# Partial sums copied into PSUM banks a stage earlier, and the w_down pieces made at other places, in a four-layer Fourier-mixing and GEGLU kernel

## The chip, the cores and the metric

The kernel runs on one core of a Trainium2 chip. The metric is the device time of one execution in microseconds; the time before is the median of three runs, 1634.65 us (1634.25 to 1635.71). The profile is of one more execution, which took 1635.97 us; from its first to its last instruction there are 1634.0 us (the span), and the mean granted TensorE clock was 0.996.

## What is computed

The input x has 2048 rows of 512 numbers. Four layers follow one another; layers 0 and 2 mix, layers 1 and 3 are a GEGLU block. The same weights serve both layers of a kind, and everything is float32.

```python
# mix (layers 0, 2), on z = layernorm(x)
a = z @ dft_hid_re.T;  b = z @ dft_hid_im.T
x = x + (dft_seq_re @ a - dft_seq_im @ b)
# GEGLU (layers 1, 3), on z = layernorm(x)
x = x + (gelu(z @ w_gate) * (z @ w_up)) @ w_down
```

dft_seq is 2048 x 2048 (real and imaginary part), dft_hid 512 x 512, w_gate and w_up 512 x 1792, w_down 1792 x 512.

## The kernel before

**Products.** A float32 operand is divided into two parts: the high part is a copy rounded to fp32r on ScalarE (L148), the low part is the difference on VectorE (L150). A product is three matmuls, high by high, high by low and low by high (`mm3`, L205, L206, L207). Only the first matmuls of layer 0 take plain float32 (L797). Large products are done in two-by-two blocks with seven block products in place of eight. For that, sums and differences of the operands are formed on VectorE (`minus` L181, `plus` L188 from SBUF), they are divided into high and low part, and the results are combined as they leave their PSUM banks: `plus` on VectorE (L185) or a copy on ScalarE (`copied`, L192). There are eight banks. Where a result begins with a sum that is known already, a bank is filled with it first: the seed, a ScalarE copy into the bank (`seed`, L199), and the matmuls add to it.

**A mix layer** has four blocks b of 512 output rows. Per block the stages are A11, A12 (two of the seven products over the sequence, 8 steps k each), S2 (products T2, T1 and T3, each a little behind the one before), the hidden-layer groups, S4 (products B22 and T4), and more hidden-layer groups (MID_HID, LATE_HID). `plan` lists the stages: A11 of all four blocks, A12 of all four, then per block S2, EARLY_HID, S4, MID_HID, LATE_HID. A stage's product with one k is `six` (six matmuls); the weights come from a stream of items through `take`, which loads and divides some items ahead. A12 begins with the seed of two banks by A11's sums; S2 begins with the seed of two banks by the sums of A11 for its block, which for b > 0 were put into DRAM and are loaded back by `fetch_sums`; the hidden-layer groups begin with the seed of four banks by the rows of x (`x_seeded`), to which the layer's result is added.

**A GEGLU layer** has two halves w of 1024 rows. It runs 14 passes n over gate and up columns (`up`), each with seven products; every pass forms h, and two passes make one pair k = 0..6 of w_down rows. The w_down products A11 and A12 of a pair are done in the passes (`beside`), the other five (S1, S2, S3, S4, A22) after them, in the order of `down_order`: the late products. In layers 1 (both halves) and 3 (first half) all seven pairs are done in this way; in layer 3's second half five pairs, and the rest by plain products.

**w_down pieces.** The w_down operands of a pair k are made once and kept in DRAM. `weight_steps` gives six steps for it: a load (L922 to L924, 0.52 MB), the sums (four of 128x256 on VectorE), and four divides (three of 128x512 and one of 128x256, on ScalarE and VectorE), whose results POOL's queue writes out (seven writes of 256 KB, L309 and L943). Seven pairs make 42 steps. The gate/up pieces are made in the same way in layer 1's first passes.

**What sets the order.** Instructions are issued per engine in a static order that a scheduler of the framework makes from the program's order and its own estimates. Some steps are hung onto it by hand: `step()` runs after each product, takes one entry from `queue`, and each `pace[0]`-th time one from `slow`. With `in_order` set (in the mix layers, but for layer 0's A11 and A12), splits, differences and seeds are issued behind the last bank read on their engine (`behind`, L141). Loads are on SP's queue, most writes on POOL's. Tiles of SBUF come from 98 slots; a load waits until the earlier reader of its slot is done.

The lines that the prediction names: L148 and L150 splits, L181 and L188 differences and sums, L192 and L185 bank reads, L199 seeds, L205 to L207 matmuls, L309 and L943 writes of pieces.

Of the kernel before, what the change touches and what calls it, by code (L numbers as in the profile page):

```python
# [20 lines left out]
NB = S // TB  # L21
NT = TB // P
# [7 lines left out]
LAG = 6  # L30
NEAR = 3, 2, 6
EARLY = 2
PACE = 9
SKEW = 2, 1
NSLOT = 98
SEVEN = {(1, 0): 7, (1, 1): 7, (3, 0): 7, (3, 1): 5}
FORE = {0: 4, 2: 4}
MADE = 5
LEAD = 3
NK = NS // 2  # L40
DOWN_PACE = 4


@with_exitstack
def fnet_geglu(ctx: ExitStack, tc: tile.TileContext, x_in, ws, wh, wgu, wdn, wdc, out):
# [86 lines left out]
    sb = Slots(slots, "s", NSLOT)  # L132
# [125 lines left out]
        for i in range(NT):  # L258
            xrows[b, i] = x_load(layer, b * NT + i)

    def x_seeded(b):

        banks = [ps8.get() for _ in range(NT)]
        for i, ps in enumerate(banks):
            t = xrows.pop((b, i))
            seed(ps, t)
            sb.put(t)
        return banks

# [175 lines left out]
    NP = NF // 2  # L445

    def down_order(layer, w):
        n = SEVEN[layer, w]
        up = [(name, k) for k in range(n) for name in ("A11", "A12")]
        if n < NP:  # L450
            late = [("S2", k) for k in range(n)] + [("S1", 0)] + [("S3", k) for k in range(n)] + [("S1", 1)]
            late += [("A22", k) for k in range(n - 1)] + [("S1", k) for k in range(2, n)]
            return up, late + [("A22", n - 1)] + [("S4", k) for k in range(n)]
        late = [("S1", k) for k in range(LEAD)] + [up.pop()]
        late += [p for k in range(n) for p in [("S2", k)] + [("S1", k + LEAD)] * (k + LEAD < n)]
        late += [("S4", k) for k in range(2)]
        for k in range(2, n):
            late += [("S3", 3 * (k - 2) // 2 + i) for i in range(1 + k % 2) if 3 * (k - 2) // 2 + i < n] + [("S4", k)]
        return up, late + [("A22", k) for k in range(n)]
# [47 lines left out]
                items.extend((F32, (wdn[f],), plain, None) for f in range(2 * SEVEN[layer + 1, w], NF))  # L507


    queue, slow, steps_done, pace = [], [], [0], [PACE]  # L510

    def step():
        if queue:
            run = queue.pop(0)
            if run is not None:
                run()
        steps_done[0] += 1
        if slow and steps_done[0] % pace[0] == 0:
            slow.pop(0)()


# [212 lines left out]
    def mix(layer):  # L734
# [14 lines left out]
        def hid_groups(b, groups):  # L749

            first, last = b not in hid, groups is LATE_HID
            if first:
                hid[b] = x_seeded(b)
                chores.extend(chores_at(b))
                hid_left[0] = 2 * ND
            if last and b + 1 < min(NB, FORE[layer]):
                fetch_sums(b + 1)  # L760
            for n, g in enumerate(groups):
                (hi, lo), w = take()
                for i in range(NT):
# [3 lines left out]
                step()  # L767
                for _ in range(-(-len(chores) // hid_left[0]) if chores else 0):
                    chores.pop(0)()
                hid_left[0] -= 1  # L770
            if last:
                for i, ps in enumerate(hid.pop(b)):
                    x_out(layer, b * NT + i, ps)

        def six(ps, name, k, start, stop, done=None):
            w = take()
# [14 lines left out]
        def a11(b):  # L791
            chain = [ps8.get() for _ in range(2)]
            for k in range(NK):
                if bare(layer, b, "A11", k):
                    t, = take()
                    for c in range(2):
                        nc.tensor.matmul(chain[c], za[k][:, c * P:(c + 1) * P], t, start=k == 0, stop=False, skip_group_check=True)  # L797
                    sb.put(t)
                    step()
                else:  # L800
                    six(chain, "B11", k, k == 0, k == NK - 1, "11" if b == NB - 1 else None)
            sums[b] = [copied(p) for p in chain]
            ps8.put(*chain)

        def a12(b):
            stream["more"] = 0
            if layer and b == 0:
                lend("x")
                lend("z")
            side = [ps8.get() for _ in range(2)]  # L810
            for c in range(2):
                seed(side[c], sums[b][c])
                if b:
                    put_away((layer, b, c), sums[b][c])
            for k in range(NK):
                six(side, "B21", k, False, k == NK - 1, "21" if b == NB - 1 else None)
            for c in range(2):
# [9 lines left out]
        def s2(b):  # L827
# [3 lines left out]
                lend("x")  # L831
            cs.update(cs_next)
            cs_next.clear()
            chain = [ps8.get() for _ in range(2)]
            for c in range(2):
                seed(chain[c], sums[b][c])
            sb.put(*sums.pop(b))
            x_banks(layer, b)
            one, three = [ps8.get() for _ in range(2)], [ps8.get() for _ in range(2)]
            sides[b] = one, three  # L840
# [2 lines left out]
            for i, k in skewed(3):  # L843
                if i == 0:
                    six(chain, "T2", k, False, k == NK - 1)
                elif i == 1:
                    six(one, "T1", k, k == 0, k == NK - 1, "T12" if last else None)
                else:
                    six(three, "T3", k, k == 0, k == NK - 1)
                if k < NK - 1:  # L850
                    continue
                if i == 0:
                    us[b] = [copied(p) for p in chain]
                    ps8.put(*chain)
                for c in range(2):
                    if i == 1:
                        v = cs[1, 2 + c] = sb.get()
                        plus(v, us[b][c], one[c])
                    elif i == 2:
                        plus(cs[1, 2 + c], cs[1, 2 + c], three[c])  # L860

        def s4(b):
# [5 lines left out]
            for i, k in skewed(2):  # L868
# [3 lines left out]
                    six(three, "T4", k, False, k == NK - 1, "T34" if last else None)  # L872
                if k < NK - 1:
                    continue
                for c in range(2):
                    if i == 0:
                        v = cs[0, 2 + c] = sb.get()
# [7 lines left out]
        for n, (b, what) in enumerate(plan(layer)):  # L885
# [17 lines left out]
        pace[0] = PACE  # L903

# [78 lines left out]
    def geglu(w, layer):  # L983
# [475 lines left out]
```

## Time and profile before

| | before |
|---|---|
| time, median of 3 runs | 1634.65 us |
| the profiled execution: time, span | 1635.97 us, 1634.0 us |
| TensorE busy | 1605.1 us (98%) |
| VectorE busy | 1135.9 us (70%) |
| ScalarE busy | 888.8 us (54%) |
| GpSimd busy | 269.3 us (16%) |
| DMA | 419.14 MB, mean 257 GB/s |
| matmuls | 7008 |

Times in the trace count from the span's start. The stages lie there as follows: layer 0 has A11 and A12 until about 96 us, block 0 until 175, block 1 until 252, block 2 until 328, block 3 until 413. Layer 1's first half has its passes until 569, its second half until 776; layer 2's A11 run from 811 to 864, its A12 to 920, its blocks to 1224; layer 3 takes the rest.

The rows of busy time overlap, since the engines work beside each other. A row of the list of waits reads: engine and its line, the line it waited for, total us, number of times, longest. A row of a table of stretches reads: from and to, length, then for PE, PEld (the weight loads of TensorE), DVE (VectorE), ACT (ScalarE) and POOL (GpSimd) the busy us and the number of instructions, the granted clock, the DMA engines' share and GB/s. A row of a timeline reads: start, duration, engine, line, operation, and in brackets the idle time ahead of it with what ended it. A row of groups reads: line, engine, operation, tiles, shapes, count, busy us and mean ns of one, then idle us ahead of them.

### The profile page before, as it was taken

What the parts mean: (1) busy time and instruction counts of PE and PEld (TensorE: products, weight loads), DVE (VectorE), ACT (ScalarE), POOL (GpSimd) and SP (SyncE); (2) the same over time, 40 slices, a digit from 0 to 9 for tenths busy, and PEclk for the clock granted to TensorE, in tenths of its full rate; (3) what the DMA queues carried; (4) which work ended last, traced back from release to release, by engine and by line L of the source; (5) the groups of instructions that cost most, each with busy time, mean ns of one, the idle gap of its engine ahead of it and who ended that gap; (6) DMA issues with size and microseconds to landing.
All of it is one profiled execution on the core that took longest, in us unless ns stands there. A gap on an engine that the chain in (4) does not pass through costs nothing. (4 is left out here: it accounts for less than half of the span.)

```text
span 1634.0 us, 22639 instructions
## 1 busy us (share of the span) xinstructions
PE 1605.1 (98%) x7008; PEld 1318.0 (81%) x7008; DVE 1135.9 (70%) x1958; ACT 888.8 (54%) x1711; POOL 269.3 (16%) x469
## 2 busy tenths in 40 slices
PE   9999999989999999999998999999999999999998
PEld 7887888868888887788786788888888888888886
DVE  7997888878787784445977958777863447744573
ACT  8855475645676653546656634655555536433460
POOL 4112131342544101100040000101401000000001
PEclk9999999999999999999999999999999999999999
DMA  9878899997988889955794776868999676895445
GB/s 359 291 260 302 314 322 316 329 327 236 307 292 255 275 277 304 252 180 174 255 302 140 257 241 206 307 203 303 257 298 308 205 213 204 275 300 187 123 148 155
DMA packets 258840, 419.14 MB, mean 257 GB/s; under 512 B 28512, under 2 KB 106592, under 8 KB 257696
## 3 DMA queue, kind: packets, MB, share of 16 engines
q1 hardware_dynamic: 234480, 336.16, 64.9%
q0 software_dynamic: 24240, 81.55, 13.8%
q8 instruction: 55, 0.90, 0.2%
q14 instruction: 65, 0.53, 0.1%
HBM read 341.31 MB, written 76.28 MB: 256 GB/s over the span
## 5 line engine op out<-in xcount | busy, mean ns | idle before, releaser
L206 PE MATMUL p<-s,s 128*128 128x512 f32 x2320 | 903.3, 390 | 2.4 <-DVE s L150 2.4
L207 PE MATMUL p<-s,s 128*128 128x512 f32 x2320 | 896.5, 390 | 0.0
L205 PE MATMUL p<-s,s 128*128 128x512 f32 x2320 | 871.9, 391 | 18.8 <-ACT s L148 9.0
L150 DVE TENSOR_TENSOR s<-s,s 128x512 fp32r<-128x512 f32 (+1 forms) x806 | 507.7, 665 | 127.8 <-ACT s L148 108.7
L148 ACT ACTIVATE s<-s 128x512 fp32r<-128x512 f32 (+1 forms) x806 | 452.4, 606 | 222.6 <-DVE s L181 63.9
L205 PEld LDWEIGHTS p<-s,s 128*128 128x128 f32 x2320 | 436.4, 188 | 115.6 <-ACT s L148 11.8
L206 PEld LDWEIGHTS p<-s,s 128*128 128x128 f32 x2320 | 436.5, 188 | 95.7 <-DVE s L150 5.5
L207 PEld LDWEIGHTS p<-s,s 128*128 128x128 f32 x2320 | 436.7, 188 | 90.8
L185 DVE TENSOR_TENSOR s<-s,p 128x512 f32<-128x512 f32 x196 | 132.6, 683 | 205.8 <-PE p L207 163.7
L181 DVE TENSOR_TENSOR s<-s,s 128x512 f32<-128x512 f32 (+1 forms) x364 | 217.9, 615 | 5.4 <-DMA s<-ws 3.0
L192 ACT ACTIVATE s<-p 128x512 f32<-128x512 f32 x233 | 133.9, 593 | 114.5 <-PE p L207 112.0
L980 ACT ACTIVATE s<-s 128x512 f32<-128x512 f32 x84 | 52.8, 630 | 71.5 <-DVE s L185 70.8
L564 POOL TENSOR_SCALAR rstd<-rstd 128x1 f32<-128x1 f32 x40 | 30.6, 764 | 281.1 <-ACT s L563 266.2
L148 ACT ACTIVATE s<-xwide 128x512 fp32r<-128x512 f32 x73 | 44.7, 625 | 49.7 <-DVE xwide L185 25.9
L994 DVE TENSOR_TENSOR s<-s,p 128x512 f32<-128x512 f32 x56 | 38.4, 685 | 34.6 <-PE p L207 31.7
L309 POOL DMA_DIRECT2D wb<-s x84 | 45.8, 546 | 94.3 <-ACT s L148 70.5
L980 ACT ACTIVATE s<-p 128x512 f32<-128x512 f32 x28 | 16.7, 598 | 76.3 <-PE p L207 72.5
L150 DVE TENSOR_TENSOR s<-xwide,s 128x512 fp32r<-128x512 f32 x73 | 49.6, 688 | 10.9 <-ACT s L148 10.0
L188 DVE TENSOR_TENSOR s<-s,s 128x512 f32<-128x512 f32 (+1 forms) x72 | 43.5, 610 | 17.2 <-DMA s<-ws 15.9
L587 ACT ACTIVATE s<-s,shift,rstd 128x512 f32<-128x512 f32 x56 | 45.0, 811 | 14.5 <-DVE shift L554 8.9
L199 ACT ACTIVATE p<-p 128x512 f32<-128x512 f32 x56 | 32.7, 584 | 36.4 <-PE p L207 27.6
L669 DVE STREAM_TRANSPOSE wide<-s 128x512 f32<-128x512 f32 x27 | 19.1, 709 | 36.3 <-ACT s L587 36.3
(104 smaller groups left out, 603.5 us busy)
## 6 DMA issues: line engine op xcount, KB each, us to landing
s<-ws SPq DMA_DIRECT2D x380, 256.0 KB, 5.3
s<-wb SPq DMA_DIRECT2D x294, 256.0 KB, 4.5
s<-wc SPq DMA_DIRECT2D x182, 256.0 KB, 4.0
s<-wh SPq DMA_DIRECT2D x118, 256.0 KB, 5.3
wb<-s POOLq DMA_DIRECT2D x98, 256.0 KB, 4.5
s<-x SPq DMA_DIRECT2D x60, 256.0 KB, 5.3
xwide<-ws SPq DMA_DIRECT2D x52, 256.0 KB, 5.0
wc<-s POOLq DMA_DIRECT2D x49, 256.0 KB, 4.7
```

Of the source, the lines that this page charges most:

```text
L148: newest["ACT"] = nc.scalar.activation(hi, src, AF.Copy)
L150: newest["DVE"] = nc.vector.tensor_tensor(lo, src, f32(hi), op=ALU.subtract)
L181: nc.vector.tensor_tensor(out, a, b, op=ALU.subtract)
L185: bank_read["DVE"] = nc.vector.tensor_tensor(out, a, b, op=ALU.add)
L188: nc.vector.tensor_tensor(out, a, b, op=ALU.add)
L192: bank_read["ACT"] = nc.scalar.activation(v, src, AF.Copy)
L205: nc.tensor.matmul(ps, ah, bh, start=start, stop=False, skip_group_check=True)
L206: nc.tensor.matmul(ps, ah, bl, start=False, stop=False, skip_group_check=True)
L207: nc.tensor.matmul(ps, al, bh, start=False, stop=stop, skip_group_check=True)
L309: nc.gpsimd.dma_start(a, f32(t))
L587: nc.scalar.activation(z, x, AF.Identity, bias=shift, scale=rstd)
L980: nc.scalar.activation(t, g, AF.Gelu_apprx_tanh)
```

## The change

Three things are done.

1. Seeds. The seeds of A12 and S2 move out of these stages into the stage before. `a12_seeded(b)` fills two banks: for block 0 at step k = 3 (SEED_AT) of the last A11, for block b + 1 at step 3 of A12 of block b. `s2_seeded(b)` does so for S2: for block 0 at step 3 of the last A12, for later blocks in the last hidden-layer group of the block before; the loads of `fetch_sums` come one group earlier. `x_seeded` fills its four banks in two halves, two at step 3 of T2 in S2, two after T2's banks are copied.
2. w_down pieces. The 42 steps are no longer in `slow`. Four of them run ahead of T2's bank read and four ahead of B22's bank read in layer 0's blocks 0, 1 and 2 (24 steps, the pieces of four pairs), none in block 3, and two in each pass n > 2 of layer 1's first half (18 steps, three pairs).
3. Late w_down operands. In the passes from n = 9 on, where all seven pairs are done, the operands of the first entries of the late list (two more with each pass) are divided already if their pair is there. The last A12 stands two places later in the late list.

```diff
+EARLY_FROM, EARLY_EACH = 8,2
-DOWN_PACE = 4
+SEED_AT = 3
+DOWN_RUNS = ((0,0,0,0),(4,4,4,0),(4,4,4,0),2)
...
-    def x_seeded(b):
-        banks = [ps8.get() for _ in range(NT)]
-        for i, ps in enumerate(banks):
+    def x_seeded(b, rows):
+        banks = []
+        for i in rows:
             t = xrows.pop((b, i))
-            seed(ps, t)
+            banks.append(ps8.get())
+            seed(banks[-1], t)
             sb.put(t)
...
-        late = [("S1", k) for k in range(LEAD)] + [up.pop()]
+        late = [("S1", k) for k in range(LEAD)]
         late += [p for k in range(n) for p in [("S2", k)] + [("S1", k + LEAD)] * (k + LEAD < n)]
+        late.insert(LEAD + 2, up.pop())
...
             if first:
-                hid[b] = x_seeded(b)
+                hid[b] = hid_banks.pop(b)
...
-            if last and b + 1 < min(NB, FORE[layer]):
-                fetch_sums(b + 1)
+            if b + 1 < NB:
+                if groups is MID_HID:
+                    fetch_sums(b + 1)
+                elif last:
+                    s2_seeded(b + 1)
...
+        def down_pieces(b, at):
+            for _ in range(DOWN_RUNS[at][b]):
+                if layer == 0 and down_making:
+                    down_making.pop(0)()
...
+                if b == FORE[layer] - 1 and k == SEED_AT:
+                    a12_seeded(0)
...
+        def a12_seeded(b):
+            side_banks[b] = [ps8.get() for _ in range(2)]
+            for c in range(2):
+                seed(side_banks[b][c], sums[b][c])
+                if b:
+                    put_away((layer, b, c), sums[b][c])
+
+        def s2_seeded(b):
+            chain_banks[b] = [ps8.get() for _ in range(2)]
+            for c in range(2):
+                seed(chain_banks[b][c], sums[b][c])
+            sb.put(*sums.pop(b))
...
-            side = [ps8.get() for _ in range(2)]
-            for c in range(2):
-                seed(side[c], sums[b][c])
-                if b:
-                    put_away((layer, b, c), sums[b][c])
+            side = side_banks.pop(b)
             for k in range(NK):
                 six(side, "B21", k, False, k == NK - 1, "21" if b == NB - 1 else None)
+                if k == SEED_AT:
+                    if b + 1 < FORE[layer]:
+                        a12_seeded(b + 1)
+                    else:
+                        s2_seeded(0)
...
-            chain = [ps8.get() for _ in range(2)]
-            for c in range(2):
-                seed(chain[c], sums[b][c])
-            sb.put(*sums.pop(b))
+            chain = chain_banks.pop(b)
...
+                if i == 0 and k == SEED_AT:
+                    hid_banks[b] = x_seeded(b, range(2))
...
                 if i == 0:
+                    down_pieces(b, 1)
                     us[b] = [copied(p) for p in chain]
                     ps8.put(*chain)
+                    hid_banks[b] += x_seeded(b, range(2, NT))
...
+                if i == 0:
+                    down_pieces(b, 2)
...
-                pace[0] = DOWN_PACE
                 for k in range(NP):
                     load, making = down_weight_steps(k)
-                    slow.extend([load] + making)
+                    down_making.extend([load] + making)
...
+            if n > 2:
+                for _ in range(DOWN_RUNS[3]):
+                    if down_making:
+                        down_making.pop(0)()
             product(n, chain[n], "S2", "T2", False, True)
...
+            if pairs == NP:
+                for name, k in down_order(layer, w)[1][:max(0, n - EARLY_FROM) * EARLY_EACH]:
+                    if k in h4:
+                        prepared(name, k)
             product(n, chain[n], "A22", "T4", False, True)
```

More of the change, by code (lines that the diff above doesn't have):

```diff
@@ L507, in fnet_geglu @@
                 items.extend((F32, (wdn[f],), plain, None) for f in range(2 * SEVEN[layer + 1, w], NF))
-    queue, slow, steps_done, pace = [], [], [0], [PACE]
+    queue, slow, steps_done, down_making = [], [], [0], []
     def step():
@@ L517, in step @@
         steps_done[0] += 1
-        if slow and steps_done[0] % pace[0] == 0:
+        if slow and steps_done[0] % PACE == 0:
             slow.pop(0)()
@@ L767, in hid_groups @@
                 step()
+                down_pieces(b, 0)
                 for _ in range(-(-len(chores) // hid_left[0]) if chores else 0):
@@ L801, in a11 @@
                     six(chain, "B11", k, k == 0, k == NK - 1, "11" if b == NB - 1 else None)
+                if b == FORE[layer] - 1 and k == SEED_AT:
+                    a12_seeded(0)
             sums[b] = [copied(p) for p in chain]
             ps8.put(*chain)
+        side_banks, chain_banks, hid_banks = {}, {}, {}
+        def a12_seeded(b):
[9 more added lines that the diff above has]
+            sb.put(*sums.pop(b))
         def a12(b):
@@ L902, in mix @@
         in_order[0] = False
-        pace[0] = PACE
     wblocks = {n: dram.tile([P, 7 * 512], F32, name=f"wb{n}") for n in range(NF)}
```

## The prediction

> **What bounds the kernel now.** I read the page's engine table first, then TensorE's list of waits, and then cut the span into the stretches where TensorE stands.
>
> ```profile
> span 1634.0 us, 22639 instructions
> PE 1605.1 (98%) x7008; PEld 1318.0 (81%) x7008; DVE 1135.9 (70%) x1958; ACT 888.8 (54%) x1711; POOL 269.3 (16%) x469
> ```
>
> TensorE is busy 98% of the span, and the change takes no matmul away. So only time in which TensorE stands or runs at a lower clock can be won: 1634.0 - 1605.1 = 29 us of idle time, and a little more around each gap, as the next rows show. The list of waits names what it stands for:
>
> ```profile
> PE p L205 <- ACT s L148: 9.0, 7, 2.6
> PE p L205 <- ACT p L199: 8.0, 4, 4.1
> ```
>
> L199 is the seed, a copy of known sums into a PSUM bank ahead of the products that add to it; four waits of 8.0 us in all are for it. L148 is the high part of a split. This is the table of stretches that hold the gaps; its columns are the stretch, its length, busy time and count for PE, PEld, DVE, ACT and POOL, the granted clock, the DMA share and GB/s.
>
> ```profile
> 128.00:135.00 7.00, 4.70 (x20) 3.35 (x19) 5.71 (x10) 6.25 (x13) 0.54 (x1) 1.00 0.51 170
> 340.00:360.00 20.00, 16.40 (x68) 12.15 (x68) 19.13 (x34) 9.58 (x16) 9.27 (x17) 1.00 0.99 313
> 360.00:376.00 16.00, 13.97 (x53) 10.61 (x52) 11.69 (x21) 9.30 (x18) 11.57 (x23) 0.89 0.88 240
> 651.00:658.00 7.00, 4.54 (x18) 2.80 (x18) 0.69 (x1) 7.00 (x23) 2.22 (x6) 1.00 1.14 243
> 777.00:800.00 23.00, 20.76 (x90) 16.34 (x89) 21.55 (x37) 15.66 (x29) 0.00 (x0) 1.00 0.77 254
> 863.00:880.00 17.00, 12.89 (x44) 10.11 (x43) 15.45 (x36) 8.33 (x16) 1.07 (x2) 0.80 0.29 93
> 880.00:894.00 14.00, 12.49 (x55) 10.01 (x54) 9.71 (x20) 8.48 (x16) 0.00 (x0) 1.00 0.38 126
> 894.00:906.00 12.00, 10.76 (x48) 8.60 (x47) 9.61 (x17) 8.48 (x16) 1.08 (x2) 1.00 0.87 279
> 906.00:920.00 14.00, 12.82 (x57) 10.26 (x57) 14.00 (x25) 8.56 (x16) 1.08 (x2) 1.00 0.79 253
> ```
>
> The first three are stages S2 and S4 of the first mix layer (layer 0), in blocks 0, 3 and 3. 651 to 658 lies in the gate/up passes of layer 1's second half, 777 to 800 in its late w_down products. The last four are the four A12 stages of layer 2. How much a gap costs is read from the largest, in TensorE's timeline (start, duration, idle before):
>
> ```profile
> 862.73 0.39 PE L205 MATMUL p<-s,s 128*128 128x512 f32 x1
> ...
> 863.86 0.39 PE L207 MATMUL p<-s,s 128*128 128x512 f32 x1
> 868.36 0.80 PE L205 MATMUL p<-s,s 128*128 128x512 f32 x1 [4.11 <-ACT p L199]
> 868.95 0.63 PE L206 MATMUL p<-s,s 128*128 128x512 f32 x1
> ...
> 874.50 0.43 PE L207 MATMUL p<-s,s 128*128 128x512 f32 x1
> 874.77 0.39 PE L205 MATMUL p<-s,s 128*128 128x512 f32 x1
> ```
>
> Ahead of the gap five starts take 1.13 us, 0.227 each. From 863.86 to 874.77 there are 16 starts, 3.6 us at that pace; they took 10.9. So 7.3 us are lost: 4.1 idle, 13 starts from 868.95 to 874.50 at 0.427 instead of 0.227 (2.6), and 0.6 for the pipeline's emptying and refilling. At full clock that last part is about 0.3 a gap, since a matmul lasts 0.39 and starts 0.227 apart, on both sides of the gap.
>
> **The change, part by part.** (1) Seeds of A12 and S2 a stage ahead. Why the wait of 4.1 us is there shows in ScalarE's timeline:
>
> ```profile
> 860.60 5.07 ACT L148 ACTIVATE s<-s 128x512 fp32r<-128x512 f32 x12
> ...
> 866.75 1.07 ACT L192 ACTIVATE s<-p 128x512 f32<-128x512 f32 x2
> 867.70 1.12 ACT L199 ACTIVATE p<-s 128x512 f32<-128x512 f32 x2
> ```
>
> A11 ended at 864.2, its bank copies (L192) stood behind splits until 866.75, and the next stage's seeds came behind the copies. In the new order the seeds of A12 block 0 need only A11 block 0, long done, and stand in the middle of A11 block 3; each next pair stands in the middle of the A12 before. The copies remain but nothing on TensorE waits for them until later. What goes: 7.3 us, and 1.51 + 0.3, 1.24 + 0.3, 1.18 + 0.3 in the next three rows (14.00 - 12.49 and so on), 4.8: **12.1 us**. The ten L199 instructions stay as many, so ScalarE's load is unchanged.
>
> What is late next is VectorE. The last four rows have 15.45 + 9.71 + 9.61 + 14.00 = 48.8 us of its work in 57; with 12.1 us out there are 44.9. If all that work were due inside the stretch, 3.9 us would come back; if enough of it is for stages after 920, none. The stretch behind has room:
>
> ```profile
> 924.00:944.00 20.00, 20.00 (x90) 16.55 (x89) 16.22 (x27) 7.78 (x15) 0.00 (x0) 1.00 0.70 228
> DVE s L150 <- ACT s L148: 5.7, 5, 2.9
> DVE s L188 <- DMA s<-ws: 2.3, 2, 2.1
> ```
>
> The two waits are VectorE's for 864 to 920. The 5.7 us are for ScalarE, which itself stands at bank reads behind TensorE; they go when TensorE doesn't stand. I take 1.0 of the 3.9, nearer the low end because the 14.00 of the last row holds splits for T1 and T2 that are used after 920. **Part 1: -11.1.**
>
> (2) Layer 0: w_down pieces out of block 3, hidden-layer seeds and S2's seeds earlier. VectorE is busy 19.13 of 20 us in 340:360, and ahead of that it had stood:
>
> ```profile
> 339.08 0.69 DVE L188 TENSOR_TENSOR s<-s,s 128x512 f32<-128x512 f32 x1 [4.04 <-DMA s<-ws]
> 340.71 0.69 DVE L188 TENSOR_TENSOR s<-s,s 128x512 f32<-128x512 f32 x1 [0.94 <-DMA s<-ws]
> 330.00:340.00 10.00, 10.00 (x46) 8.29 (x45) 4.81 (x8) 3.77 (x8) 0.57 (x2) 1.00 1.03 408
> L943 POOL DMA_DIRECT2D wc<-s x3: 539/539/539, 290.5 to 375.9; - x3
> ```
>
> Two sums came 5.0 us late for loads of the sequence weights, with the DMA engines full at 408 GB/s, and VectorE did not catch up before 360. The L943 row is of 252 to 413: three of seven w_down pieces are made in blocks 2 and 3. One piece is a load of 0.52 MB and seven writes of 256 KB, 2.36 MB; three are 7.1 MB and 15 steps on VectorE. By the order of the new kernel's instructions these are gone from the stretch, four pieces are made between blocks 0 and 2, ahead of bank reads at which VectorE waits anyway, and S2's first products don't wait for a seed. Lost now: 2.30 + 0.6 in 128:135; 3.60 + four gaps by 0.3 in 340:360; and in 360:376
>
> ```profile
> 366.90 0.73 PE L205 MATMUL p<-s,s 128*128 128x512 f32 x2 [1.21 <-ACT s L148]
> 368.45 0.49 PE L205 MATMUL p<-s,s 128*128 128x512 f32 x1 [0.83 <-ACT s L148]
> 369.54 0.63 PE L206 MATMUL p<-s,s 128*128 128x512 f32 x1
> 372.52 0.53 PE L207 MATMUL p<-s,s 128*128 128x512 f32 x1
> ```
>
> 2.03 + 0.6 and nine starts at 0.427 (1.8): 2.9 + 4.8 + 4.4 = 12.1. Bounds: nothing of it left, or only 128:135 won. S4 opens on splits that come behind S2's last bank reads in either kernel, so I leave 1.9 standing at that boundary. **Part 2: -10.2.**
>
> The Trainium skill, TensorE: Matmul & The Clock Gate, "What's actually happening", says that the clock is halved after at least one idle window of about 3.4 us. The trace agrees at 863.86 (4.11 us), but nine half-speed starts also followed 1.21 and 0.83 us of idle time. By the rule the 1.9 us left standing would stay 1.9; by these rows they could carry another 1.8.
>
> (3) Late w_down operands split in the passes, A12's last product two places later. 777:800 loses 23.00 - 20.76 = 2.2 of idle time in two gaps, 2.9 with refilling, while VectorE is busy 21.55 of 23. Ten splits of it move in front of 800, and further back. Between 0 and 2.9 I take 2.4. **Part 3: -2.4.** 651:658 (2.5 idle) waits for norm terms, which are unchanged: 0.
>
> (4) What comes into layer 1's first passes. Their rows, two passes each, and VectorE's and ScalarE's forms there:
>
> ```profile
> 439.70:461.40 21.70, 21.70 (x97) 17.98 (x96) 16.20 (x32) 14.56 (x32) 9.54 (x19) 1.00 1.04 361
> 461.40:483.20 21.80, 21.80 (x98) 18.06 (x97) 18.12 (x35) 15.12 (x32) 9.46 (x18) 1.00 0.77 275
> ...
> 526.70:548.50 21.80, 21.80 (x97) 18.05 (x97) 14.47 (x26) 11.38 (x21) 7.01 (x13) 1.00 1.02 325
> ...
> sum 129.00, PE 129.00 PEld 106.83 DVE 98.17 ACT 83.33 POOL 44.44; mean PE 21.50 PEld 17.80 DVE 16.36 ACT 13.89 POOL 7.41
> L150 DVE TENSOR_TENSOR s<-s,s 128x512 fp32r<-128x512 f32 x55 | 37.0, 689 | 25.3 <-ACT s L148 23.1 <-PE p L206 1.4 <-ACT s L980 0.7
> L181 DVE TENSOR_TENSOR s<-s,s 128x256 f32<-128x256 f32 x27 | 11.4, 421 | 0.2
> L148 ACT ACTIVATE s<-s 128x512 fp32r<-128x512 f32 x58 | 34.9, 623 | 7.0 <-DVE s L994 3.4 <-PE p L207 2.8 <-PE p L206 0.6
> ```
>
> TensorE never stands here now. A piece is four 256-wide sums (4 x 0.42), three 512-wide splits (3 x 0.69) and one 256-wide (0.42): 4.2 us of VectorE, and 2.3 of ScalarE. Three pieces and ten early splits (6.9 and 6.2) make VectorE 98.2 + 12.5 + 6.9 = 117.6 of 129 us (91%) and ScalarE 83.3 + 6.8 + 6.2 = 96.3 (75%). What hides them is VectorE's 31 us of idle time; 25.3 of it are waits for ScalarE's half of a split, and so not all free. The 21 writes stand on POOL's queue with the gate/up pieces' writes, and loads on SP's queue wait for the slots they free. 7.1 MB over nine passes of 10.9 us add 72 GB/s; the busiest row with new pieces, 526.70:548.50, goes from 325 to 397, under the 408 of 330:340. Bounds: 0, and 5.0, which is what late loads cost VectorE at 339 to 341, once. I take **+2**, between them.
>
> The Trainium skill, DMA: Bandwidth & Descriptors, "Where 436 GB/s comes from", says that the HBM side binds transfers between HBM and SBUF at about 358 GB/s a core. The trace shows 408 for 10 us, so I don't go by it; by it 39 GB/s over 21.8 us, 0.85 MB, would come 2.4 us late, and the sum would be that much worse.
>
> The sum: -11.1 - 10.2 - 2.4 + 2 = -21.7 against the profiled execution's own 1635.97 us (1634.0 of span and 2.0 around it), 1614.3. The median of the runs, 1634.65, is 1.3 lower, so I say **1613**.
>
> **Rivals.** (A) VectorE takes over in layer 2's A12 stages: the 3.9 us all come back, and the 2.3 of its load waits besides, 6.2 in place of 1.0: 1618. For it speak 14.00 of 14.00 in 906:920; against it the work that is due later. (B) The change does not do in block 3 what it says: the DMA engines, at shares of 0.88 to 1.03 from 330 to 376, are what is late, not VectorE's load, and the weights' sums wait all the same. Then of 9.2 us in 340:376 only some 3 go, 6 fewer with the left boundary counted once: 1619. Against it: 7.1 MB leave just these blocks. (C) Slower: the pieces in the passes find no slots. Their sums stand at VectorE's head waiting for a load that waits for POOL's writes, and the splits of the current pass stand behind them. The price a pass is that of 340:360, where 5.0 us of such waits became 4.8 on TensorE; nine passes, 43 us against 23.7 of gain: 1654. It decides from 2.6 us a pass. For it: DMA shares of 1.04 and 1.02 in two of the rows. Against it: VectorE's idle time of 31 us, and SP's order, which has each load about a pass ahead of its sums.
>
> **How the numbers follow.** Forecast 0.68, spread over 1606 to 1617: 1606 if parts 1 to 3 leave nothing standing and part 4 costs nothing (1634.65 - 27.2 = 1607, and 1 for unlisted small gaps). A 0.12, B 0.12, C 0.08. Range **1606 to 1620**: it takes in the forecast but for its edges, A and most of B, and leaves out C. A measurement here tells 0.2%, 3.3 us, from no change. A and B are faster too: faster 0.89; C weaker than priced, near its deciding point, 0.03 for the same; slower 0.08.
>
> **What would show it.** Right: no L199 in TensorE's list of waits and a granted clock of 1.00 near 864; under 2 us idle in S2 and S4 of layer 0's block 3, with the load wait of VectorE gone; no gap near 780; in layer 1's first passes under 3 us of idle TensorE. Wrong: L148 and L150 as releasers in layer 2's A12 in place of L199 (A); a load wait of VectorE again near 335 (B); TensorE idle in pass after pass between 445 and 550, behind L181 waiting for loads (C).

## The result, and the profile after

The changed kernel takes 1619.62 us (median of six runs, 1617.86 to 1625.86) against 1634.81 us for the kernel before in the same six rounds. The ratio is 0.9912, 95% interval 0.9893 to 0.993: a gain of 14.4 us on 1634.65. Forecast were 21.7 us, 1613, in a range of 1606 to 1620; the median of the runs lies at the upper edge, the time by the ratio (1620.3) just past it. The sign was right, and a third of the gain is missing. The profiled execution is the fastest of the six, 1617.86 us. Some lines moved in the file: splits are now L150 and L152, the seed L201, the bank reads L194 and L187, sums L183 and L190, the multiplication of gate and up L1028, the w_down loads L956 to L958.

The page of the kernel after, and the three longest rows of TensorE's list of waits (after):

```profile
span 1615.7 us, 22644 instructions
PE 1598.9 (99%) x7008; PEld 1317.2 (82%) x7008; DVE 1133.3 (70%) x1958; ACT 885.4 (55%) x1711; POOL 260.9 (16%) x469
```

```profile
PE p L207 <- DMA s<-wc: 4.2, 3, 2.1
PE p L207 <- DVE s L1028: 3.6, 1, 3.6
PE p L207 <- ACT s L150: 2.2, 1, 2.2
```

The rows left out are of 1.4 us and less, and none is for a seed: the seed is gone from the list. Waits for ScalarE's half of a split fell from 9.0 to 2.2 us. Two rows are new: a wait for weights from DMA, and one of 3.6 us for a multiplication. The stretches of before, and the new ones (after):

```profile
128.00:135.00 7.00, 7.00 (x32) 5.82 (x31) 7.00 (x13) 7.00 (x15) 0.00 (x0) 1.00 0.39 114
340.00:360.00 20.00, 20.00 (x90) 16.58 (x89) 16.67 (x29) 10.75 (x20) 11.91 (x22) 1.00 1.05 276
360.00:376.00 16.00, 16.00 (x72) 13.27 (x71) 13.90 (x24) 9.54 (x18) 2.17 (x4) 1.00 0.92 271
428.00:446.00 18.00, 14.42 (x57) 11.52 (x56) 10.10 (x21) 8.94 (x19) 5.44 (x12) 0.91 0.94 332
566.00:574.00 8.00, 5.79 (x25) 4.17 (x24) 8.00 (x14) 4.86 (x9) 0.00 (x0) 1.00 1.06 370
...
774.00:784.00 10.00, 8.49 (x37) 6.53 (x36) 8.59 (x16) 7.35 (x15) 0.00 (x0) 1.00 1.07 371
...
864.00:884.00 20.00, 20.00 (x90) 16.59 (x89) 19.69 (x44) 14.06 (x27) 1.07 (x2) 1.00 0.59 188
884.00:904.00 20.00, 20.00 (x90) 16.35 (x89) 19.80 (x33) 11.19 (x23) 1.07 (x2) 1.00 0.82 257
```

The first three rows and the last two have no idle TensorE left; that is everything that the seeds and layer 0 could give. Rows four and five, in layer 1's passes (428) and right behind them (566), hold what came in its place. Row six, in the late products of the second half (774), holds a gap that was there before (777:800): TensorE waits 1.51 us at 779.65 for w_down weights, where it waited 1.68 us at 780.47 for a split. The gap near 438 begins on VectorE. Its timeline, and two rows of SP's (after):

```profile
432.05 0.68 DVE L187 TENSOR_TENSOR s<-s,p 128x512 f32<-128x512 f32 x1
439.53 0.43 DVE L190 TENSOR_TENSOR s<-s,s 128x256 f32<-128x256 f32 x1 [6.79 <-DMA s<-wdc]
```

```profile
427.02 0.35 SPq L958 DMA_DIRECT2D s<-wdc  x1
...
429.98 0.33 SPq L957 DMA_DIRECT2D s<-wdc  x1
```

The first w_down pair of the passes has its last load issued at 429.98, and its sums stood at VectorE's head (next in its fixed order) from 432.7 to 439.5. So the load was issued 2.7 us before VectorE came to the sums, and they could start 9.5 us after it was issued. The DMA engines' share from 429.9 to 439.6 is 1.04, at 389 GB/s. The other two pairs of the passes made no wait: their last loads were issued at 461.67 and 500.89, 9.8 and 3.5 us ahead of their sums, with DMA shares of 0.99 (459 to 472) and 0.96 (499 to 505). Why the first load took so much longer to land than the third is not traced. Behind the first sums stood the multiplication (L1028) that empties a PSUM bank, and TensorE waited for that bank (after):

```profile
437.64 0.39 PE L209 MATMUL p<-s,s 128*128 128x512 f32 x1
441.61 0.80 PE L207 MATMUL p<-s,s 128*128 128x512 f32 x1 [3.58 <-DVE s L1028]
442.20 0.63 PE L208 MATMUL p<-s,s 128*128 128x512 f32 x1
...
444.76 0.51 PE L208 MATMUL p<-s,s 128*128 128x512 f32 x1
445.11 0.39 PE L209 MATMUL p<-s,s 128*128 128x512 f32 x1
```

For the comparisons below, "lost" is the time by which the starts of TensorE's matmuls lie further apart than 0.227 us, summed over a stretch of one profiled execution. In all, 37.6 us were lost before and 21.8 after.

| lost, us | layer 0, 100 to 420 | layer 1's first passes | behind them, to 600 | 643 to 661 | 770 to 810 | layer 2's A12 | near 1380 |
|---|---|---|---|---|---|---|---|
| before | 12.5 | 0 | 0.5 | 3.3 | 2.8 | 12.1 | 0.5 |
| after | 0.6 | 5.4 | 2.8 | 4.4 | 1.9 | 0 | 0.9 |

The span fell by 18.3: 15.8 of it is this, 1.7 are a shorter tail behind the last matmul, and 0.8 is not placed. The tail was 4.1 to 6.8 us from kernel to kernel in the runs below, with its instructions in the same order, so I count it as spread.

### The profile page after: what moved, and what is told of

Same layout as the page of the kernel before. It is cut to its first block, busy times and chain, and to the rows that moved or that the text cites. A ratio compares the mean times of both kernels' runs of the same rounds, so it can differ in the third digit from the quotient of the medians.

```text
span 1615.7 us, 22644 instructions
## 1 busy us (share of the span) xinstructions
PE 1598.9 (99%) x7008; PEld 1317.2 (82%) x7008; DVE 1133.3 (70%) x1958; ACT 885.4 (55%) x1711; POOL 260.9 (16%) x469
## 5 line engine op out<-in xcount | busy, mean ns | idle before, releaser
L150 ACT ACTIVATE s<-s 128x512 fp32r<-128x512 f32 (+1 forms) x809 | 454.9, 607 | 264.0 <-DVE s L183 72.9
L152 DVE TENSOR_TENSOR s<-s,s 128x512 fp32r<-128x512 f32 (+1 forms) x809 | 510.8, 669 | 121.0 <-ACT s L150 102.4
L187 DVE TENSOR_TENSOR s<-s,p 128x512 f32<-128x512 f32 x188 | 127.5, 685 | 175.6 <-PE p L209 146.5
L183 DVE TENSOR_TENSOR s<-s,s 128x512 f32<-128x512 f32 (+1 forms) x374 | 224.8, 619 | 7.9 <-PE p L208 3.7
L194 ACT ACTIVATE s<-p 128x512 f32<-128x512 f32 x232 | 134.0, 594 | 112.0 <-PE p L209 107.6
L1014 ACT ACTIVATE s<-s 128x512 f32<-128x512 f32 x84 | 52.7, 629 | 69.1 <-DVE s L187 66.9
L568 POOL TENSOR_SCALAR rstd<-rstd 128x1 f32<-128x1 f32 x40 | 22.3, 556 | 347.4 <-ACT s L567 331.9
L152 DVE TENSOR_TENSOR s<-xwide,s 128x512 fp32r<-128x512 f32 x71 | 48.3, 687 | 33.9 <-ACT s L150 33.6
L1028 DVE TENSOR_TENSOR s<-s,p 128x512 f32<-128x512 f32 x56 | 38.4, 686 | 31.5 <-PE p L209 28.2
L190 DVE TENSOR_TENSOR s<-s,s 128x512 f32<-128x512 f32 (+1 forms) x68 | 41.1, 613 | 16.5 <-DMA s<-wdc 9.8
L150 ACT ACTIVATE s<-xwide 128x512 fp32r<-128x512 f32 x71 | 43.1, 621 | 17.2 <-DVE xwide L183 6.6
L201 ACT ACTIVATE p<-p 128x512 f32<-128x512 f32 x56 | 32.7, 585 | 27.9 <-PE p L209 27.7
L565 ACT ACTIVATE s<-s 128x512 f32<-128x512 f32 x33 | 20.7, 627 | 42.1 <-DMA s<-x 22.2
```

The lines of the kernel that those rows point to most:

```text
L150: newest["ACT"] = nc.scalar.activation(hi, src, AF.Copy)
L152: newest["DVE"] = nc.vector.tensor_tensor(lo, src, f32(hi), op=ALU.subtract)
L183: nc.vector.tensor_tensor(out, a, b, op=ALU.subtract)
L187: bank_read["DVE"] = nc.vector.tensor_tensor(out, a, b, op=ALU.add)
L190: nc.vector.tensor_tensor(out, a, b, op=ALU.add)
L194: bank_read["ACT"] = nc.scalar.activation(v, src, AF.Copy)
```

## The experiments

The theory after this comparison: parts 1 and 2 gained their full 24 us, and the w_down pairs in layer 1's passes give part of it back, because a load stands too close ahead of its sums at VectorE's head. Rivals: the passes are simply too full (VectorE, DMA or slots); the late products' new order makes weights late. Ratios are to the kernel before on the same chip, with the 95% interval; its median there was 1636 to 1638.

**Which part does what.** Four kernels take parts alone or away. `seeds_only` is the kernel before with part 1; `pieces_only` with the w_down pieces alone; `late_only` with early splits and the new place of the last A12.

```diff
 # seeds_only, against the changed kernel (and part three undone)
+                pace[0] = 4
-                    down_making.extend([load] + making)
+                    slow.extend([load] + making)
 # pieces_only, against the kernel before
-                    slow.extend([load] + making)
+                    down_making.extend([load] + making)
 # late_only, against the kernel before
-        late = [("S1", k) for k in range(LEAD)] + [up.pop()]
+        late = [("S1", k) for k in range(LEAD)]
+        late.insert(LEAD + 2, up.pop())
```

> The kernel before with the first part alone, the seeds a stage earlier; w_down pieces made at the old pace in layer 0, late operands as before. If the seeds alone carry layer 2's gain of 12.1 us and 2.9 at the boundary of layer 0's block 0, and block 3 of layer 0 is lost to the w_down pieces: about 1620, with 8 to 9 us still lost in S2 and S4 of block 3. Rival (block 3 was lost to its own late seeds and copies): nothing is lost there, about 1611.

Measured: 0.9887 (0.9863 to 0.9912), 1619.67 us. As much as the whole change: the two intervals overlap. Layer 2's A12 lost 1.1 in place of 12.1; layer 0 still 7.2. The rows of seeds_only for block 3:

```profile
340.00:360.00 20.00, 18.02 (x72) 14.17 (x71) 13.02 (x21) 5.36 (x9) 14.36 (x28) 0.91 0.98 274
360.00:380.00 20.00, 19.12 (x84) 15.21 (x83) 16.71 (x28) 13.59 (x26) 5.42 (x10) 1.00 0.94 283
```

> The kernel before with the second part alone: w_down pieces in layer 0's blocks 0 to 2 and in layer 1's first passes, seeds and late operands as before. If the pieces gave layer 0's block 3 its gain, 340 to 376 loses 1 to 3 us in place of 9; and the passes lose 5 us near 438 and up to 5 more at their end: 1634 to 1636, no gain. Rival (the passes' waits are made by the early splits or by the new seeds): no gap near 438, about 1627.

Measured: 1.0034 (1.0018 to 1.0049), 1642.9 us: slower than before. Layer 0 lost 4.6 in place of 12.5, but the passes 6.9 and the stretch behind them 10.8. The first two of TensorE's waits below are those of before, the third is the gap in the passes (pieces_only):

```profile
PE p L205 <- ACT p L199: 6.9, 4, 3.0
PE p L205 <- ACT s L148: 6.4, 6, 2.2
PE p L205 <- DVE s L1000: 5.1, 1, 5.1
```

So the gap belongs to the pieces, without seeds and without early splits.

> The kernel before with the third part alone: early splits of late operands and the last A12 product two places later. By the forecast the waits near 780 go: 2 to 3 us faster than before, about 1632. If the new place of the product makes the weights behind it late also without the pieces, three waits for weights of 1 to 2 us stand after the passes and the gain is under 1 us.

Measured: 0.9967 (0.9952 to 0.9983), 1631.53 us. Near 780 still 2.0 were lost and behind the first passes 0.8: the gain isn't there. The profile has it in layer 2's A12 (6.3 lost in place of 12.1), though no line of that stage is changed; why ScalarE reaches the seeds earlier there is not traced. Layer 0, where no line is changed either, lost 14.9 in place of 12.5.

> The changed kernel without its third part: no early splits of late operands, the last A12 product at its old place. Both theories of the late weights say that the waits for weights go (4.9 us with refilling). The old waits for splits near 780 (2.2 us idle) come back if part three was what removed them: then 1 to 2 us faster than the changed kernel. If pieces and seeds alone had removed them, 4 to 5 us faster.

Measured: 0.9947 (0.9927 to 0.9967), 1629.11 us: slower than the changed kernel by 5.7 (0.0035 x 1635), where both theories said faster; the intervals just overlap. With part three undone, 11.1 us are lost behind the first passes, in place of 2.8, and 4.3 from 782 to 790, in place of 1.9: a wait of 2.28 us for a split is back there (785.53), with half-speed starts behind it. Behind the first passes ScalarE's longest wait is for the turned input of the next half (no_late, 538 to 585):

```profile
ACT s L150 <- DMA s<-t: 8.3, 2, 4.6
```

TensorE's own longest wait in that stretch, 2.81 us at 575.16, is put down to another load, of gate/up weights.

**The two halves of part three.** `order_back` keeps the early splits and puts the A12 back; `order_only` drops the early splits and keeps the new place.

```diff
 # order_only, against the changed kernel
-            if pairs == NP:
-                for name, k in down_order(layer, w)[1][:max(0, n - EARLY_FROM) * EARLY_EACH]:
-                    if k in h4:
-                        prepared(name, k)
```

> The changed kernel with the last A12 product back at its old place in the late list; the early splits of late operands stay. Theory 1 (the new place of that product makes the weights of the product behind it late): the three waits of TensorE for w_down weights (2.1, 1.5 and 0.6 us at 573, 780 and 1373) go, and since the splits are early the old waits near 780 don't come back: 4 to 5 us faster than the changed kernel. Rival (the early splits hold slots, and the loads of weights wait for slots): the waits for weights stay, within 1 us of the changed kernel.

> The changed kernel without the early splits; the last A12 product at its new place. With both parts of step three the ratio was 0.9912, with neither 0.9947, with the early splits alone 0.9952. If the new place alone is what helps: 0.991 to 0.992, and the early splits are worth nothing. If it needs both: 0.994 to 0.996.

Measured: order_back 0.9952 (0.9937 to 0.9967), order_only 0.9974 (0.9953 to 0.9994); lost behind the passes 10.2 and 8.9. The theory that the A12's new place is what makes the weights late falls: without it things are worse, and TensorE still waits 2.4 us for w_down weights. Such waits are in the profile of every kernel that has either half of part three (1.5 to 6.6 us in all) and of none that has neither (the kernel before, seeds_only, pieces_only, no_late, mix_pieces_no_late). With the pairs in the passes it takes both halves to come to 0.9912; why neither helps alone stays open.

**The late load.**

```diff
 # load_ahead, against the changed kernel
-            if n > 2:
-                for _ in range(DOWN_RUNS[3]):
+            if n > 1:
+                for _ in range(DOWN_RUNS[3] if n > 2 else 1):
```

> The changed kernel, but the 18 w_down steps of layer 1's first half begin one step earlier, with one step in pass 2: each of the three loads then stands a pass ahead of its sums instead of in the same pass. Theory 1 (one load of a w_down pair is asked for too late, and its sums stand at VectorE's head): the gap of TensorE near 438 us goes (3.6 us idle, 5.7 us lost with the half-speed starts behind it), and the time falls by 5 to 6 us against the changed kernel, to about 1614. Rival (the DMA engines are full between 418 and 446 us, so something else is late there or a pass later): a gap of like size appears elsewhere between 430 and 550 us, and the time stays within 2 us of the changed kernel's 1620.

Measured: 0.9894 (0.9876 to 0.9912), 1619.89 us, against 0.9912 (0.9893 to 0.993) for the changed kernel: not told apart. The gap near 438 is gone, as the theory said: the first sums run at 434.64 without a wait. The gain of 5 to 6 us did not come. 6.5 us are lost from 557 to 575 in place of 2.8, which is the rival's in kind, though it named 430 to 550 (load_ahead):

```profile
428.00:446.00 18.00, 18.00 (x82) 14.88 (x81) 14.01 (x27) 13.48 (x28) 8.14 (x15) 1.00 1.09 316
...
566.00:580.00 14.00, 11.33 (x41) 8.31 (x40) 13.43 (x23) 7.30 (x14) 0.00 (x0) 0.88 1.04 362
```

> The changed kernel as it is, once more, beside the others: ratio 0.990 to 0.993 as in the first measurement, and the gap near 438 of 4 to 7 us in this profile too, if the late load belongs to the order and not to that one execution.

Measured: 0.9917 (0.99 to 0.9934), 1622.5 us; 7.2 lost at 441 to 450. The gap belongs to the order. TensorE's idle time was 5.32 here and 3.58 in the first profile. VectorE waited 8.54 us ahead of the same sums; the profile puts that down to a load of x, but the sums read w_down tiles alone, and their last load was issued at 435.33, 9.7 us ahead of them (again):

```profile
447.10 0.80 PE L207 MATMUL p<-s,s 128*128 128x512 f32 x1 [5.32 <-DVE s L1028]
```

**Other places for the pairs.** All these keep parts one and three.

```diff
 # mix_pieces (mix_pieces_no_late: with part three undone)
-DOWN_RUNS = ((0,0,0,0),(4,4,4,0),(4,4,4,0),2)
+DOWN_RUNS = ((0,0,0,0),(7,7,7,0),(7,7,7,0),0)
 # hid_pieces
+DOWN_RUNS = ((1,1,0,0),(5,4,4,0),(5,4,4,0),0)
 # one_pair
+DOWN_RUNS = ((0,0,0,0),(6,6,6,0),(6,6,6,0),2)
 # pair_later: six pairs in layer 0, load in pass 5, a step each in passes 7 to 11
+            if n == 5 or n > 6:
 # hid_b0
+DOWN_RUNS = ((1,0,0,0),(6,6,5,0),(6,6,5,0),0)
```

> The changed kernel with all 42 w_down steps in layer 0: seven ahead of T2's bank read and seven ahead of B22's in blocks 0, 1 and 2 (six pairs' worth a bank read more than before, none in block 3), and none in layer 1's passes. Theory (the 18 steps in the passes cost what they save in block 3 of layer 0: loads late at 438, and at the passes' end): the gap near 438 goes, the waits from 550 to 600 shrink to those of the kernel with seeds alone (under 1 us), block 3 of layer 0 stays free, and the time is 6 to 8 us under the changed kernel, about 1612. Rival (blocks 0 to 2 have no room for 18 more steps): 4 us or more are lost between 100 and 330, and the time stays near 1620.

> The same without the third part (no early splits of late operands, the last A12 product at its old place). If part three is worth what was forecast, this is 2 to 3 us slower than with it; if its early splits and its order only trade waits for splits against waits for weights, the two are equal within 1 us.

Measured: 0.9866 (0.9845 to 0.9888), 1616.14 us, and without part three 0.9879 (0.9854 to 0.9903). By the ratios this is 7.5 us faster than the changed kernel, as the theory said, and next to nothing (0.2) is lost in the passes or behind them. But block 3 did not stay free: 8.1 are lost in layer 0, most of it at 357 to 370, later than the rival had it. And part three, worth 5.7 us with pairs in the passes, is worth too little here to tell.

> All 42 w_down steps in layer 0, but 16 of them one by one in the hidden-layer groups of blocks 0 and 1, and four (five in block 0) ahead of each bank read in blocks 0 to 2: fewer before each bank read than in the fastest kernel so far, which lost 7 us in blocks 2 and 3 (332 to 370). If the steps crowd the bank reads there, these 7 us shrink to 1 to 2 and the ratio falls to about 0.983 (1609). Rival (the DMA engines are full from 140 on, and every piece moved in front of block 3 makes its loads late): the loss stays, ratio 0.986 to 0.988.

Measured: 0.9877 (0.9856 to 0.9898). Block 3 loses nothing; block 1 now loses 4.0 at 189 to 195 and block 2 2.4 at 288, so the ratio is the rival's.

> Six w_down pairs in layer 0 (six steps ahead of each bank read of blocks 0 to 2) and one pair in layer 1's passes 3 to 5 in place of three pairs in passes 3 to 11. If the late first load is most of the price (theory H): the gap near 440 comes back, 4 to 6 us, and nothing at the passes' end; ratio 0.989 to 0.991. If the price goes with the number of pairs: a third of it, 3 us, ratio about 0.988.

Measured: 0.9881 (0.9865 to 0.9898). 9.0 us lost at 441 to 453, 0.6 behind the passes. The ratio is what the second theory said; the profile has the gap that theory H said, larger than forecast, with 2.2 lost in layer 0 where mix_pieces lost 8.1. So near 440 the first pair is the price, not the number of pairs. VectorE's wait and TensorE's (one_pair):

```profile
444.98 0.42 DVE L190 TENSOR_TENSOR s<-s,s 128x256 f32<-128x256 f32 x1 [9.91 <-DMA s<-wdc]
```

```profile
447.66 0.80 PE L207 MATMUL p<-s,s 128*128 128x512 f32 x1 [5.94 <-DVE s L1028]
```

> Six w_down pairs in layer 0 (six steps ahead of each bank read of blocks 0 to 2) and one in layer 1's passes: its load in pass 5, its five steps of engine work in passes 7 to 11, one each. With the same pair in passes 3 to 5, load and sums together, 9.0 us were lost at 441 to 453. Theory H (a load too close ahead of its sums, at a time of full DMA engines): nothing is lost near 440, under 1.5 us elsewhere in the passes, 6 to 9 us faster than with the pair in passes 3 to 5, ratio 0.983 to 0.985. Rival (a pair costs wherever it stands in the passes): ratio 0.987 to 0.989.

Measured: 0.9869 (0.9846 to 0.9892), 1615.53 us: just under the rival's ratio, and further from theory H's, though the interval holds both. Nothing is lost near 440, as theory H said, but 5.5 at 565 to 574, where ScalarE waits 5.5 us for the turned input (pair_later, 545 to 580):

```profile
ACT s L150 <- DMA s<-t: 5.5, 2, 4.9
```

So a pair has two prices: at the beginning of the first one the load behind which VectorE stands, and, where its steps stand in the last passes, a loss behind them. The first is shown: the gap goes with the load in load_ahead and pair_later and is back in one_pair. The second is in no_late, load_ahead and pair_later alike, and its cause is not shown. Waits for the turned input of 3.6 to 4.0 us are also in mix_pieces, hid_pieces and hid_b0, which lose 0.4 and less there; TensorE's own wait in pair_later, 2.81 us at 570.60, is again put down to gate/up weights.

> All 42 w_down steps in layer 0: eight in the hidden-layer groups of block 0, six ahead of each bank read in blocks 0 and 1, five in block 2. With seven ahead of each bank read 6 to 8 us were lost at 357 to 372, with six under 1.5. If that loss is due to what stands in block 2: under 2 us there, ratio 0.983 to 0.985. If the pieces crowd layer 0 wherever they stand: 4 us or more lost between 100 and 375, ratio 0.986 to 0.988.

Measured: 0.9832 (0.981 to 0.9853), 1610.14 us: 13 us (0.008 x 1636) under the changed kernel, and the fastest of all. The two profiled spans differ by only 7.3, since the changed kernel's is that of its fastest run; its six runs lie 8 us apart, the four of hid_b0 0.7. Eight steps in block 0's hidden-layer groups, six or five ahead of a bank read, none in block 3 or in the passes (hid_b0):

```profile
340.00:360.00 20.00, 20.00 (x90) 16.58 (x89) 13.85 (x23) 7.57 (x14) 11.52 (x22) 1.00 1.06 276
360.00:376.00 16.00, 15.77 (x70) 12.71 (x69) 15.57 (x27) 12.21 (x23) 2.13 (x4) 1.00 0.98 286
428.00:446.00 18.00, 18.00 (x81) 14.89 (x80) 12.66 (x24) 12.18 (x26) 8.30 (x17) 1.00 1.08 355
...
566.00:580.00 14.00, 13.94 (x62) 11.24 (x61) 14.00 (x24) 10.26 (x19) 0.00 (x0) 1.00 1.07 373
```

**What of a pair costs.** On top of mix_pieces, layer 1's passes get one cost alone: 21 second writes of gate/up pieces to unused DRAM (dma_add), 18 unused splits of 128x512 (vector_add), both, or four slots taken away (slots4).

```diff
 # dma_add
+                    if again is not None:
+                        kept(again, t)
 # vector_add
+            if (layer, w) == (1, 0) and 2 < n < 12:
+                for _ in range(2):
+                    sb.put(*split_slot(u[n]))
 # slots4
+            if (layer, w) == (1, 0) and n == 3:
+                held_back.extend(sb.get() for _ in range(4))
```

> All w_down pieces in layer 0 (as in the fastest kernel so far, ratio 0.9866 to before), and in layer 1's first passes the written gate/up pieces of three columns (6, 9, 12) are written a second time to unused DRAM: 21 more writes of 256 KB, no more work on VectorE or ScalarE and no more loads. Theory D (the pieces' traffic makes the loads of those passes late): waits come at the passes' end, 4 to 8 us, ratio 0.989 to 0.992. Theory V (the pieces' work on VectorE is what costs): the time stays within 1.5 us of the same kernel without the writes.

> All w_down pieces in layer 0, and in layer 1's passes 3 to 11 two more splits of 128x512 each, whose results are not used: 18 x 0.69 = 12.4 us of VectorE (as much as three w_down pairs cost) and 11 us of ScalarE, no DMA. Theory D: within 1.5 us of the same kernel without them, ratio about 0.987. Theory V: 4 to 8 us slower, waits of TensorE for splits between 440 and 570.

> All w_down pieces in layer 0; in layer 1's passes both additions together, the 21 second writes of 256 KB and the 18 unused splits. If traffic and engine work cost only together (theory D+V): 4 to 8 us slower than the kernel without additions, ratio 0.989 to 0.992. If neither matters (theory H: only the sums at VectorE's head that wait for a load of their own): within 1.5 us, ratio 0.986 to 0.988.

> All w_down pieces in layer 0; in layer 1's passes 3 to 10 four SBUF slots are taken and left unused, as many as the raw tiles of a w_down pair hold. Theory S (the pieces make loads wait for slots): 4 to 8 us slower than without, loads and splits late from 550 to 590, ratio 0.989 to 0.992. Theories D+V and H: within 1.5 us.

Measured: dma_add 0.9864 (0.9843 to 0.9885), vector_add 0.9874 (0.9859 to 0.9888), slots4 0.9877 (0.9862 to 0.9891), all within mix_pieces' interval. both_add 0.992 (0.9902 to 0.9939): clear of them by 7 to 9 us. By the times, neither work, traffic nor slots cost anything alone that can be told; work and traffic together do. That they cost only together is not shown. both_add's profile loses 2.9 us at 572 to 575, and so does dma_add's; it loses 6.1 at 649 to 659 (3.1 in mix_pieces), and vector_add's loses 6.4 there. In layer 0, where the five kernels have the same lines, dma_add lost 3.8 and vector_add 3.5 but mix_pieces 8.1, both_add 7.7 and slots4 10.4: single profiles scatter by more than the prices sought, and the rest of both_add's loss isn't placed.

## Why the prediction was right in sign and too large

- **Part 1, -11.1: right, measured -12.1.** L199 is gone as a releaser. Of the 3.9 us that VectorE might give back nothing came: it is busy 19.69 and 19.80 of 20 us at 864 to 904, and its splits are in time. Rival A did not come.
- **Part 2, -10.2: right, -11.9 with the seeds and pieces together**, the 1.9 left standing at block 3's boundary was not needed. The seeds alone won 5.3 of it, the pieces alone 7.9; the forecast gave block 3 to the pieces. VectorE's 5.0 us of load waits at 335 to 340 are 0.2 now. Rival B did not come.
- **Part 3, -2.4: the wait that it takes away was right, the size was not.** 777:800 went from 2.8 lost to 1.9, so 0.9. The wait for a split is gone there (it is back in no_late), but a wait for w_down weights of 1.5 us stands in its place, which the sum put at nothing; another lost 0.4 more near 1380. Part three has a use that was not forecast: with pairs in the passes it is worth 5.7 us, which the profiles have mostly behind them (no_late).
- **Part 4, +2, bounds 0 and 5.0: the step that failed.** In the changed kernel's two profiles 5.4 and 7.2 us are lost near 440 and 2.8 and 2.4 behind the passes, 8 to 10 in all, where the sum has 2 and its upper bound 5.0. The sum of busy time (91% of VectorE) was weighed, and it is not what makes the gap: vector_add adds as much and costs nothing that can be told; with the traffic as well it does cost (both_add), but without a gap near 440. What I named for rival C, a sum at VectorE's head waiting for its load, came, but once and not in nine passes. The premise that failed is "SP's order, which has each load about a pass ahead of its sums". By the change's own lines a pair's load and its sums are the two steps of one and the same pass; the first pair's last load was issued 2.7 us before VectorE came to the sums (429.98 and 432.7), and they waited 6.8 us for it. Why 2.3 us more are lost behind the passes than before stays open.
- Not in the sum: 643 to 661 lost 4.4 in place of 3.3, with idle time unchanged (12.00 - 9.58 = 2.4 against 2.5):

```profile
644.00:656.00 12.00, 9.58 (x35) 6.97 (x35) 1.83 (x3) 11.55 (x37) 3.29 (x9) 0.86 1.12 271
```

Counted with the measured sizes by the table: -11.9 + 5.4 + 2.3 + 1.1 - 0.9 - 12.1 + 0.4 = -15.7. Against the forecast's -21.7, part 4 is 5.7 worse, part 3 1.9 and the unlisted stretch 1.1, while parts 1 and 2 are 2.7 better. The table is of two profiled executions, which are 18.1 us apart; that its sum lies near the -15.2 between the medians proves nothing.

## What to carry to other kernels

Work that is moved into idle time of an engine with a static order can cost what its first instruction waits for, and all that stands behind it: ask when its load is issued and how full the DMA engines are then, not only how much idle time there is. Seeds that need only old results belong into the middle of the stage before, where nothing stands behind them. When a change has several parts, try each alone: here one gave the whole gain, one was a loss by itself, and the same steps at other places gave 13 us more.

## What the hardware showed beside

Half-speed starts follow short idle times irregularly. After 2.18 us of idle time at 649.79, and another 0.24, starts were slow until 653.4 in the changed kernel (first fence). After 2.07 us at the same place, and another 0.37, they were slow until 657.6 in load_ahead (second):

```profile
649.79 1.22 PE L207 MATMUL p<-s,s 128*128 128x512 f32 x2 [2.18 <-ACT s L150]
650.80 0.63 PE L208 MATMUL p<-s,s 128*128 128x512 f32 x1
...
652.96 0.61 PE L207 MATMUL p<-s,s 128*128 128x512 f32 x1 [0.24 <-ACT s L194]
```

```profile
650.03 0.73 PE L207 MATMUL p<-s,s 128*128 128x512 f32 x2 [2.07 <-ACT s L150]
651.35 0.63 PE L209 MATMUL p<-s,s 128*128 128x512 f32 x1
...
656.78 0.63 PE L209 MATMUL p<-s,s 128*128 128x512 f32 x1
```

The difference, 6.2 against 4.4 us lost, is as large as some of the parts here. After 2.09 us of idle time at 572.96 in the changed kernel none was slow. The Trainium skill, TensorE: Matmul & The Clock Gate, "What's actually happening", says that the window is free-running and the count of slow matmuls varies from run to run. The fences are of two kernels and no test of that; the count varies between them, and in the changed kernel's second profile it is about as in its first. The Trainium skill's idle window of about 3.4 us is longer than any of these gaps.

The DMA engines moved 398 GB/s over 22 us in dma_add without a wait of TensorE (dma_add):

```profile
440.00:462.00 22.00, 22.00 (x99) 18.22 (x98) 16.88 (x32) 17.39 (x40) 12.67 (x24) 1.00 1.05 398
```
